# Key tiles transposed as fp32 pairs of bf16, with the order of TensorE's work pinned, in a decode attention kernel

**Chip, cores, metric.** One core of a Trainium2 chip. The metric is the device time of one execution in microseconds; executions are compared with those of the kernel before on the same chip. All runs quoted are of the state "fast".

## The reference, cut

```python
# A: B=4, Sq=1, D=512, 32 heads of 128, cache 8192 long, window W = 2048, all bf16
q = (xn @ wq)                                    # one query row per (batch, head): 128 pairs
k, v = k_cache[:, :, -2048:, :], v_cache[:, :, -2048:, :]
p = softmax(q @ k^T * 128**-0.5)
attn = (p @ v) @ wo
# B: a small MLP on the same 4 rows (w1..w4);  out = x + attn + mlp
```

The keys of one (batch, head) pair are 2048 x 128 bf16, 512 KB: 128 such tiles, 67.1 MB. The values are as much again. With 4.2 MB of wq, 4.2 MB of wo and the MLP's weights the core reads 146.5 MB. The score matmuls of this kernel sum over the partition dimension, so each key tile is transposed first, to bring the head dimension there.

## The kernel before, the parts concerned

```python
KV_BUFS, KTT_BUFS, STG_BUFS = 12, 16, 4       # key/value tiles, transposed halves, PSUM slots
Qm = qmpool.tile([P, NPAIR, QG], BF)          # per pair: 128x32, the query in one column, else 0

def emit_scores(h):                           # 16 matmuls, 4 rounds of 4 column strips (b)
    for sb in range(NSB):                     # NSB = 4 blocks of 512 keys
        c0 = sb * SBW
        sl, off = divmod(c0, SLW)
        for b in range(Bb):
            j = QG * b + h
            nc.tensor.matmul(S_ps[QG*b:QG*(b+1), c0:c0+SBW], lhsT=Qm[:, j, :],
                             rhs=ktT_tiles[(h, b)][sl][:, off:off+SBW],
                             start=(h == 0), stop=(h == Hq-1), tile_position=(0, QG*b))
    ...
for h in range(Hq):
    for b in range(Bb):
        kt = kvpool.tile([P, NCH, Dh], BF, name="kv")
        nc.sync.dma_start(out=kt[:], in_=kwin[b, h].rearrange("(p c) d -> p c d", c=NCH))
        slots = []
        for sl in range(NSLOT):               # 2 slots of 8 transposes
            stg = stgpool.tile([P, SLW], BF, name="stg")            # PSUM
            for cc in range(TPS):
                c = sl * TPS + cc
                nc.tensor.transpose(stg[:, cc*P:(cc+1)*P], kt[:, c, :], ident[:])
            ktT = kttpool.tile([P, SLW], BF, name="ktT")
            evac(ktT[:], stg[:])              # VectorE and ScalarE, 3:2
            slots.append(ktT)
        ktT_tiles[(h, b)] = slots
    if h - SCORE_LAG >= 0:                    # SCORE_LAG = 1
        emit_scores(h - SCORE_LAG)
# ... softmax over S_ps, then the value stage: o_ps <- PT, vt; combine; project with wo
```

The text is not the order in which TensorE gets the instructions: the framework reorders them when it builds the program.

Of the kernel before, what the change touches and what calls it, by code (L numbers as in the profile page):

```python
# [8 lines left out]
BF = mybir.dt.bfloat16  # L9
F32 = mybir.dt.float32  # L10
PSUM = bass.MemoryType.PSUM
ACTF = mybir.ActivationFunctionType
ALU = mybir.AluOpType
AX = mybir.AxisListType
# [5 lines left out]
STG_BUFS = 4  # L20
SCORE_LAG = 1
INCLUDE_TOKEN_MIX = True
TAIL_VSTAT_HEADS = 1
MLP_STAGE_AT = (10, 18, 44, 60)

# [2 lines left out]
def kernel(  # L28
# [14 lines left out]
    nc = tc.nc  # L43
    P = 128
    Bb, Sq, D = A_x.shape
    _, Hkv, Sk, Dh = A_k_cache.shape
    Hq = A_wq.shape[1] // Dh
    F = B_w3.shape[1]
    W = min(4096, max(256, Sk // 4))
    assert Sq == 1 and Dh == P and Hq == Hkv and Bb * Hq == P and D % P == 0  # L50
    assert W % P == 0
    NCH = W // P
    KD = D // P
    scale = float(Dh) ** -0.5
    NPAIR = Bb * Hq
    QG = P // Bb
    assert QG == 32 and Hq == QG
    SBW = min(512, W)
    NSB = W // SBW
    TPS = min(8, NCH)  # L60
    NSLOT = NCH // TPS
    SLW = TPS * P
# [3 lines left out]
    kwin = A_k_cache[:, :, Sk - W:Sk, :]  # L66
# [4 lines left out]
    def open_pool(**kw):  # L71
        cm = tc.tile_pool(**kw)
        return cm, cm.__enter__()

    def close_pool(cm):
        cm.__exit__(None, None, None)

    consts = ctx.enter_context(tc.tile_pool(name="consts", bufs=1))
    small = ctx.enter_context(tc.tile_pool(name="small", bufs=1))
    kvpool = ctx.enter_context(tc.tile_pool(name="kv", bufs=KV_BUFS))  # L80
    kttpool = ctx.enter_context(tc.tile_pool(name="ktt", bufs=KTT_BUFS))
    qmpool = ctx.enter_context(tc.tile_pool(name="qm", bufs=1))
# [5 lines left out]
    ident = consts.tile([P, P], BF)  # L88
    make_identity(nc, ident[:])
    eps_t = consts.tile([P, 1], F32)  # L90
    nc.vector.memset(eps_t[:], LN_EPS)
    Qm = qmpool.tile([P, NPAIR, QG], BF)
    nc.gpsimd.memset(Qm[:], 0.0)

    x_sb = small.tile([Bb, D], BF)
# [59 lines left out]
    stg_cm, stgpool = open_pool(name="stg", bufs=STG_BUFS, space=PSUM)  # L155
    ps0_cm, ps0 = open_pool(name="ps0", bufs=1, space=PSUM)
    xnT = small.tile([P, KD, Bb], BF)
    transpose_interleaved(xnT, xn_bf[:], Bb, KD, P, ps0, "xnT_ps")
    q_ps = ps0.tile([P, Hq * Bb], F32, name="q_ps")
    for h in range(Hq):  # L160
        for ic in range(KD):
            nc.tensor.matmul(q_ps[:, h * Bb:(h + 1) * Bb], lhsT=wq_sb[:, ic, h * Dh:(h + 1) * Dh],  # L162
                             rhs=xnT[:, ic, :], start=(ic == 0), stop=(ic == KD - 1))
    qm_diag = bass.AP(tensor=Qm.tensor, offset=Qm.offset,
                      ap=[list(Qm.ap[0]), [QG * QG, Bb], [QG + 1, Hq]])
    nc.vector.tensor_copy(out=qm_diag, in_=q_ps[:].rearrange("p (h b) -> p b h", b=Bb))  # L166
    close_pool(ps0_cm)
    close_pool(wq_cm)

    S_cm, spool = open_pool(name="S", bufs=1, space=PSUM)  # L170
    S_ps = spool.tile([P, W], F32, name="S_ps")

    order = [(i // Bb, i % Bb) for i in range(NPAIR)]
    evac_idx = [0]

    def evac(dst, src):
        k = evac_idx[0] % 5
        evac_idx[0] += 1
        if k in (0, 2, 4):
            nc.vector.tensor_copy(out=dst, in_=src)  # L180
        else:
            nc.scalar.copy(out=dst, in_=src)  # L182

    ktT_tiles = {}

    def emit_scores(h):
        for sb in range(NSB):
            c0 = sb * SBW
            sl, off = divmod(c0, SLW)
            for b in range(Bb):  # L190
                j = QG * b + h
                nc.tensor.matmul(S_ps[QG * b:QG * (b + 1), c0:c0 + SBW], lhsT=Qm[:, j, :],  # L192
                                 rhs=ktT_tiles[(h, b)][sl][:, off:off + SBW],
                                 start=(h == 0), stop=(h == Hq - 1), tile_position=(0, QG * b))
        for b in range(Bb):
            del ktT_tiles[(h, b)]

    for h in range(Hq):
        for b in range(Bb):
            kt = kvpool.tile([P, NCH, Dh], BF, name="kv")  # L200
            nc.sync.dma_start(out=kt[:], in_=kwin[b, h].rearrange("(p c) d -> p c d", c=NCH))
            slots = []
            for sl in range(NSLOT):
                stg = stgpool.tile([P, SLW], BF, name="stg")
                for cc in range(TPS):
                    c = sl * TPS + cc
                    nc.tensor.transpose(stg[:, cc * P:(cc + 1) * P], kt[:, c, :], ident[:])  # L207
                ktT = kttpool.tile([P, SLW], BF, name="ktT")
                evac(ktT[:], stg[:])
                slots.append(ktT)  # L210
            ktT_tiles[(h, b)] = slots
        if h - SCORE_LAG >= 0:
            emit_scores(h - SCORE_LAG)
    for h in range(max(0, Hq - SCORE_LAG), Hq):
        emit_scores(h)
# [9 lines left out]

    if INCLUDE_TOKEN_MIX:
        w1_sb = wpool.tile([P, KD, D], BF)
# [17 lines left out]
        weight_dma_at = {0: [dma_w3, dma_w4]}  # L245

    mx = smpool.tile([P, 1], F32)
    nc.vector.tensor_reduce(out=mx[:], in_=S_ps[:], axis=AX.X, op=ALU.max)  # L248
    nbias = smpool.tile([P, 1], F32)
    nc.vector.tensor_scalar(out=nbias[:], in0=mx[:], scalar1=-scale, scalar2=None, op0=ALU.mult)  # L250
    E = smpool.tile([P, W], F32)
    rowsum = smpool.tile([P, 1], F32)
    nc.scalar.activation(out=E[:], in_=S_ps[:], func=ACTF.Exp, bias=nbias[:], scale=scale, accum_out=rowsum[:])  # L253
    rinv = smpool.tile([P, 1], F32)
    nc.vector.reciprocal(out=rinv[:], in_=rowsum[:])
    Pn = smpool.tile([P, W], BF)
    nc.vector.tensor_scalar(out=Pn[:], in0=E[:], scalar1=rinv[:], scalar2=None, op0=ALU.mult)  # L257
    PT = smpool.tile([P, NCH, P], BF)
    for sl in range(NSLOT):
        ptp = stgpool.tile([P, SLW], BF, name="stg")  # L260
        for cc in range(TPS):
            c = sl * TPS + cc
            nc.tensor.transpose(ptp[:, cc * P:(cc + 1) * P], Pn[:, c * P:(c + 1) * P], ident[:])  # L263
        evac(PT[:, sl * TPS:(sl + 1) * TPS, :], ptp[:].rearrange("p (c j) -> p c j", j=P))
    close_pool(S_cm)
    close_pool(stg_cm)

# [5 lines left out]
    def mlp_stage1():  # L273
        if not INCLUDE_TOKEN_MIX:
            return
        xnn0 = small.tile([Bb, D], F32)
        layernorm(xnn0[:], xn[:], Bb)
        xnn0_bf = small.tile([Bb, D], BF)
        nc.vector.tensor_copy(out=xnn0_bf[:], in_=xnn0[:])
        xnn0T = small.tile([P, KD, Bb], BF)  # L280
        transpose_interleaved(xnn0T, xnn0_bf[:], Bb, KD, P, psB, "tpB")
        h1_ps = psB.tile([Bb, D], F32, name="mm512")
        for ic in range(KD):
            nc.tensor.matmul(h1_ps[:], lhsT=xnn0T[:, ic, :], rhs=w1_sb[:, ic, :], start=(ic == 0), stop=(ic == KD - 1))
        h1 = small.tile([Bb, Sq, D], BF)
        nc.scalar.activation(out=h1[:, 0, :], in_=h1_ps[:], func=ACTF.Gelu_apprx_tanh)
        st["h1"] = h1

    def mlp_stage2():
        if INCLUDE_TOKEN_MIX:  # L290
            h1 = st["h1"]
            g = small.tile([Bb, Sq, D], BF)
            nc.vector.memset(g[:], 0.0)
            cq = D // 4
            for s in range(Sq):
                for blk, sh in enumerate((-1, +1, -2, +2)):
                    ss = s + sh
                    if 0 <= ss < Sq:
                        nc.vector.tensor_copy(out=g[:, s, blk * cq:(blk + 1) * cq], in_=h1[:, ss, blk * cq:(blk + 1) * cq])
            gT = small.tile([P, KD, Bb], BF)  # L300
            transpose_interleaved(gT, g[:, 0, :], Bb, KD, P, psB, "tpB")
            hs_ps = psB.tile([Bb, D], F32, name="mm512")
            for ic in range(KD):
                nc.tensor.matmul(hs_ps[:], lhsT=gT[:, ic, :], rhs=w2_sb[:, ic, :], start=(ic == 0), stop=(ic == KD - 1))
            nc.vector.tensor_tensor(out=x1[:], in0=xn[:], in1=hs_ps[:], op=ALU.add)
        else:
            nc.vector.tensor_copy(out=x1[:], in_=xn[:])
        xnn = small.tile([Bb, D], F32)
        layernorm(xnn[:], x1[:], Bb)
        xnn_bf = small.tile([Bb, D], BF)  # L310
        nc.vector.tensor_copy(out=xnn_bf[:], in_=xnn[:])
        st["xnn_bf"] = xnn_bf
# [14 lines left out]
    def mlp_stage4():  # L327
# [3 lines left out]
        for fc in range(FCH):  # L331
# [15 lines left out]
                          in_=r32[:, 0:VG].unsqueeze(2).to_broadcast([P, VG, P]))  # L347
# [25 lines left out]
    for i in range(NPAIR):  # L373
        h, b = order[i]
        j = QG * b + h
# [4 lines left out]
        nc.sync.dma_start(out=vt[:], in_=vwin[b, h].rearrange("(p c) d -> p c d", c=NCH))  # L380
        if h >= Hq - TAIL_VSTAT_HEADS:
            if b == 0:
                oT_dir = otps_pool.tile([P, Bb], F32, name="oT_ps")
            for c in range(NCH):
                nc.tensor.matmul(oT_dir[:, b:b + 1], lhsT=vt[:, c, :], rhs=PT[:, c, j:j + 1],
                                 start=(c == 0), stop=(c == NCH - 1))
            if b == Bb - 1:
                head_epilogue_project(h, oT_dir)
        else:
# [3 lines left out]
            for g in range(NVG):  # L393
                nc.tensor.matmul(o_ps[QG * b:QG * b + VG, :], lhsT=PT[:, g * VG:(g + 1) * VG, j],  # L394
                                 rhs=vt[:, g * VG:(g + 1) * VG, :],
                                 start=(g == 0), stop=(g == NVG - 1), tile_position=(0, QG * b))
# [39 lines left out]
```

## Time and profile before

| | before |
|---|---|
| time, median of 6 runs | 396.59 us (395.27 to 399.32) |
| profiled span | 394.5 us |
| first to last key transpose | 16.4 to 208.3 us |
| last score ends, first value matmul starts | 210.1, 221.0 us |

The key stage goes from 16 to 210 us, softmax to 221, the value stage from there. A stage's limit is read from GB/s and from what the DMA's issue queue waits for.

### The profile page before, as it was taken

To read this page: it belongs to the slowest core of one execution; us is meant where nothing else is said; L and a number is where in the kernel's file an instruction comes from. 1 tells how busy PE (TensorE), PEld (TensorE's weight loads), DVE (VectorE), ACT (ScalarE), POOL (GpSimd) and SP (SyncE) were. 2 spreads that over 40 slices of the span, in tenths; PEclk is the share of its full clock that TensorE was granted. 3 is DMA by queue.
4 is the path that set the end of the run, shared out by engine and by line. 5 is a ranking of instruction groups with operands and counts; after the bars stand their busy time and mean duration, and the time that the engine had idled before them with its cause. 6 is when DMAs were issued, how large, how long until landed. Compare 5 with 4: busy or idle time off the path is not lost.

```text
span 394.5 us, 8101 instructions
## 1 busy us (share of the span) xinstructions
PE 304.7 (77%) x3416; PEld 178.0 (45%) x3416; DVE 188.0 (48%) x287; ACT 120.0 (30%) x149; POOL 4.3 (1%) x7
## 2 busy tenths in 40 slices
PE   0699999999999999999992865767466665666664
PEld 0666666666666766766761412222122222222222
DVE  5254555555555555555554444242544444444432
ACT  1155555554554564654554221100000000000000
POOL 4000000000000000000000000000000000000000
PEclk9999999999999999999998675855655555799996
DMA  8999999999999999999999599999999999999992
GB/s 326 412 408 407 408 406 407 367 331 365 335 375 356 333 357 358 328 362 354 339 405 387 207 403 393 408 372 389 410 402 410 407 410 410 407 410 410 407 410 112
DMA packets 43059, 147.00 MB, mean 373 GB/s; under 512 B 4264, under 2 KB 9744, under 8 KB 42768
## 3 DMA queue, kind: packets, MB, share of 16 engines
q1 hardware_dynamic: 43016, 146.49, 97.3%
q8 instruction: 26, 0.43, 0.4%
q14 instruction: 9, 0.07, 0.1%
q10 hardware_dynamic: 8, 0.00, 0.0%
HBM read 146.48 MB, written 0.00 MB: 371 GB/s over the span
## 4 chain that ended last, share of the span: by engine, by line
PE 67%; DVE 15%; DMA 14%; ACT 2%; issue 1%; DVEq 0%; ACTq 0%; SPq 0%
PE stg L207 30%; PE S_ps L192 15%; PE o_ps L394 13%; DMA kv<-in_A_v_cache_dram 10%; DVE o_sum L362 6%; DVE Dm L360 4%; DVE ktT L180 3%; PE oT_ps L364 3%; DMA wq_sb<-in_A_wq_dram 3%; PE mm L333 1%; PE y_ps L370 1%; PE q_ps L162 1%; PE mm L322 1%; DVE mx L248 1%; ACT E L253 1%
## 5 line engine op out<-in xcount | busy, mean ns | idle before, releaser
L180 DVE COPY ktT<-stg 128x1024 bf16<-128x1024 bf16 x154 | 104.1, 690 | 88.1 <-PE stg L207 80.4
L207 PEld LDWEIGHTS <-kv 128*128 128x128 bf16 x2048 | 116.2, 99 | 44.4 <-DMA kv<-in_A_k_cache_dram 27.9
L207 PE MATMUL stg<-ident,kv 128*128 128x128 bf16 x2048 | 135.7, 221 | 0.0
L182 ACT COPY ktT<-stg 128x1024 bf16<-128x1024 bf16 x102 | 102.2, 1012 | 99.5 <-PE stg L207 99.5
L394 PE MATMUL o_ps<-kv,PT 128*4 128x512 bf16 x496 | 83.4, 536 | 5.3 <-DMA kv<-in_A_v_cache_dram 4.8
L192 PE MATMUL S_ps<-ktT,Qm 128*32 128x512 bf16 x512 | 67.4, 385 | 5.2 <-DVE ktT L180 4.4
L360 DVE TENSOR_TENSOR Dm<-o_ps,maskD 128x512 f32<-128x512 f32 x31 | 21.4, 691 | 73.2 <-PE o_ps L394 73.2
L364 PE MATMUL oT_ps<-Sel,o_sum 128*128 128x4 f32 x62 | 15.7, 323 | 51.3 <-DVE o_sum L362 51.3
L369 ACT CAST oT_sb<-oT_ps 128x4 bf16<-128x4 f32 x32 | 5.2, 163 | 155.1 <-PE oT_ps L364 152.6
L364 PEld LDWEIGHTS oT_ps<-Sel,o_sum 128*128 128x128 f32 x62 | 13.0, 261 | 72.2 <-DVE o_sum L362 72.2
L394 PEld LDWEIGHTS <-PT 128*4 128x4 bf16 x496 | 23.7, 101 | 41.4 <-issue 35.3
L362 DVE TENSOR_REDUCE o_sum<-Dm 128x128 f32<-128x512 f32 x31 | 31.6, 1018 | 1.0
L192 PEld LDWEIGHTS <-Qm 128*32 128x32 bf16 x512 | 14.0, 94 | 18.7 <-issue 6.7
L370 PE MATMUL y_ps<-wo_sb,oT_sb 128*4 128x512 bf16 x32 | 17.3, 540 | 2.1 <-ACT oT_sb L369 2.1
L392 DVE MEMSET o_ps<- 128x512 f32 x31 | 15.0, 485 | 3.4 <-DVE PT L180 0.2
L162 PE MATMUL q_ps<-xnT,wq_sb 128*128 128x4 bf16 x128 | 3.6, 166 | 7.5 <-DMA wq_sb<-in_A_wq_dram 7.5
L263 PE MATMUL stg<-ident,Pn 128*128 128x128 bf16 x16 | 1.9, 312 | 7.5 <-DVE Pn L257 7.5
L162 PEld LDWEIGHTS <-wq_sb 128*128 128x128 bf16 x128 | 3.5, 104 | 7.6 <-DMA wq_sb<-in_A_wq_dram 7.6
L370 PEld LDWEIGHTS <-oT_sb 128*4 128x4 bf16 x32 | 3.2, 101 | 5.5 <-ACT oT_sb L369 5.5
L263 PEld LDWEIGHTS <-Pn 128*128 128x128 bf16 x16 | 1.6, 147 | 8.0 <-DVE Pn L257 8.0
L333 PE MATMUL mm<-w_sb,g3T 128*4 128x512 bf16 (+1 forms) x11 | 4.9, 611 | 0.0
L166 DVE CAST Qm<-q_ps 128x128 bf16<-128x128 f32 x1 | 0.7, 718 | 8.4 <-PE q_ps L162 8.4
(66 smaller groups left out, 49.7 us busy)
## 6 DMA issues: line engine op xcount, KB each, us to landing
kv<-in_A_k_cache_dram SPq DMA_DIRECT2D x128, 512.0 KB, 6.1
kv<-in_A_v_cache_dram SPq DMA_DIRECT2D x128, 512.0 KB, 10.1
wq_sb<-in_A_wq_dram SPq DMA_DIRECT2D x1, 4096.0 KB, 12.1
wo_sb<-in_A_wo_dram SPq DMA_DIRECT2D x4, 1024.0 KB, 11.1
w_sb<-in_B_w_dram SPq DMA_DIRECT2D x1, 1376.0 KB, 9.3
w_sb<-in_B_w_dram SPq DMA_DIRECT2D x1, 1280.0 KB
w_sb<-in_B_w_dram SPq DMA_DIRECT2D x2, 512.0 KB, 9.6
w_sb<-in_B_w_dram SPq DMA_DIRECT2D x1, 96.0 KB, 9.1
```

What stands on the lines that cost most here:

```text
L162: nc.tensor.matmul(q_ps[:, h * Bb:(h + 1) * Bb], lhsT=wq_sb[:, ic, h * Dh:(h + 1) * Dh], rhs=xnT[:, ic, :], start=(ic == 0), stop=(ic == K ...
L180: nc.vector.tensor_copy(out=dst, in_=src)
L182: nc.scalar.copy(out=dst, in_=src)
L192: nc.tensor.matmul(S_ps[QG * b:QG * (b + 1), c0:c0 + SBW], lhsT=Qm[:, j, :], rhs=ktT_tiles[(h, b)][sl][:, off:off + SBW], start=(h == 0), ...
L207: nc.tensor.transpose(stg[:, cc * P:(cc + 1) * P], kt[:, c, :], ident[:])
L333: nc.tensor.matmul(h2_ps[:], lhsT=g3T[:fw, fc, :], rhs=w4_sb[:fw, fc, :], start=(fc == 0), stop=(fc == FCH - 1))
L360: nc.vector.tensor_tensor(out=Dm[:], in0=o_ps[:], in1=maskD[:], op=ALU.mult)
L362: nc.vector.tensor_reduce(out=o_sum[:], in_=Dm[:].rearrange("p (m d) -> p d m", m=VG), axis=AX.X, op=ALU.add)
L364: nc.tensor.matmul(oT_ps[:], lhsT=o_sum[:], rhs=Sel[:], start=True, stop=True)
L370: nc.tensor.matmul(y_ps[:], lhsT=oT_sb[:], rhs=wo_sb[:, h, :], start=(h == 0), stop=(h == Hq - 1))
L392: nc.vector.memset(o_ps[:], 0.0)
L394: nc.tensor.matmul(o_ps[QG * b:QG * b + VG, :], lhsT=PT[:, g * VG:(g + 1) * VG, j], rhs=vt[:, g * VG:(g + 1) * VG, :], start=(g == 0), sto ...
```

## The change

The intent: read two neighbouring bf16 as one fp32 word, so that a key tile takes 8 fp32 transposes instead of 16. The head dimension then comes out split: partition i of a transposed tile holds elements 2i and 2i+1 of one key chunk (i < 64) or of the next (i >= 64), interleaved. The scores therefore use 64 rows, a step of two elements, and a query permuted to match. The diff's core (setup, masks and softmax views cut):

```diff
+    ident32 = consts.tile([P, P], F32)
+    make_identity(nc, ident32[:])
+    ... PermE, built from ident; Qm of twice the size
+    for e in range(2):
+        nc.tensor.matmul(qx_ps[:, e, :], lhsT=PermE[:, e, :], rhs=q_bf[:], start=True, stop=True)
...
+        def emit_scores(h):
+            for sl in range(NSLOT):
+                for e in range(2):
+                    for c2 in range(2):
+                        for b in range(Bb):
+                            ...
+                            rhs = src[HP*c2:HP*(c2+1), :].rearrange("i (x e) -> i x e", e=2)[:, :, e]
+                            col0 = c2 * SW2 + sl * NW
+                            tc.keep_in_program_order(nc.tensor.matmul(S_ps[QG*b:QG*(b+1), col0:col0+NW],
+                                             lhsT=Qm[HP*c2:HP*(c2+1), e, j, :], rhs=rhs,
+                                             start=(h == 0 and e == 0), stop=(h == Hq-1 and e == 1),
+                                             tile_position=(HP*c2, QG*b)))
...
+            kt32 = kt[:].rearrange("p c d -> p (c d)").bitcast(F32)
+            ...
+                    tc.keep_in_program_order(nc.tensor.transpose(stg[:, dc*P:(dc+1)*P],
+                                             kt32[:, cc*P:(cc+1)*P], ident32[:]))
```

Note the two `keep_in_program_order`: transposes and scores are also pinned to the order of the text.

More of the change, by code (lines that the diff above doesn't have):

```diff
@@ L22 @@
 INCLUDE_TOKEN_MIX = True
+PAIR_TRANSPOSE = True
 TAIL_VSTAT_HEADS = 1
@@ L91 @@
     nc.vector.memset(eps_t[:], LN_EPS)
-    Qm = qmpool.tile([P, NPAIR, QG], BF)
+    HP = P // 2
+    if PAIR_TRANSPOSE:
+        assert NCH % 2 == 0
+        ident32 = consts.tile([P, P], F32)
+        make_identity(nc, ident32[:])
+        PermE = consts.tile([P, 2, P], BF)
+        id_eo = ident[:].rearrange("p (x two) -> p two x", two=2)
+        for e in range(2):
+            for c2 in range(2):
+                nc.vector.tensor_copy(out=PermE[:, e, c2 * HP:(c2 + 1) * HP], in_=id_eo[:, e, :])
+        Qm = qmpool.tile([P, 2, NPAIR, QG], BF)
+    else:
+        Qm = qmpool.tile([P, NPAIR, QG], BF)
     nc.gpsimd.memset(Qm[:], 0.0)
@@ L163 @@
                              rhs=xnT[:, ic, :], start=(ic == 0), stop=(ic == KD - 1))
-    qm_diag = bass.AP(tensor=Qm.tensor, offset=Qm.offset,
-                      ap=[list(Qm.ap[0]), [QG * QG, Bb], [QG + 1, Hq]])
-    nc.vector.tensor_copy(out=qm_diag, in_=q_ps[:].rearrange("p (h b) -> p b h", b=Bb))
+    if PAIR_TRANSPOSE:
+        q_bf = small.tile([P, Hq * Bb], BF)
+        nc.vector.tensor_copy(out=q_bf[:], in_=q_ps[:])
+        qx_ps = ps0.tile([P, 2, Hq * Bb], F32, name="qx_ps")
+        for e in range(2):
+            nc.tensor.matmul(qx_ps[:, e, :], lhsT=PermE[:, e, :], rhs=q_bf[:], start=True, stop=True)
+            qm_diag = bass.AP(tensor=Qm.tensor, offset=Qm.offset + e * NPAIR * QG,
+                              ap=[list(Qm.ap[0]), [QG * QG, Bb], [QG + 1, Hq]])
+            nc.vector.tensor_copy(out=qm_diag, in_=qx_ps[:, e, :].rearrange("p (h b) -> p b h", b=Bb))
+    else:
+        qm_diag = bass.AP(tensor=Qm.tensor, offset=Qm.offset,
+                          ap=[list(Qm.ap[0]), [QG * QG, Bb], [QG + 1, Hq]])
+        nc.vector.tensor_copy(out=qm_diag, in_=q_ps[:].rearrange("p (h b) -> p b h", b=Bb))
     close_pool(ps0_cm)
@@ L170 @@
     S_cm, spool = open_pool(name="S", bufs=1, space=PSUM)
-    S_ps = spool.tile([P, W], F32, name="S_ps")
     order = [(i // Bb, i % Bb) for i in range(NPAIR)]
@@ L184 @@
     ktT_tiles = {}
-    def emit_scores(h):
-        for sb in range(NSB):
-            c0 = sb * SBW
-            sl, off = divmod(c0, SLW)
-            for b in range(Bb):
-                j = QG * b + h
-                nc.tensor.matmul(S_ps[QG * b:QG * (b + 1), c0:c0 + SBW], lhsT=Qm[:, j, :],
-                                 rhs=ktT_tiles[(h, b)][sl][:, off:off + SBW],
-                                 start=(h == 0), stop=(h == Hq - 1), tile_position=(0, QG * b))
-        for b in range(Bb):
-            del ktT_tiles[(h, b)]
@@ L198, with s_col, transpose_tile, emit_scores @@
-    for h in range(Hq):
-        for b in range(Bb):
-            kt = kvpool.tile([P, NCH, Dh], BF, name="kv")
-            nc.sync.dma_start(out=kt[:], in_=kwin[b, h].rearrange("(p c) d -> p c d", c=NCH))
+    if PAIR_TRANSPOSE:
+        NDC = NCH // 2
+        DPS = min(4, NDC)
+        NSLOT = NDC // DPS
+        NW = DPS * P
+        SW2 = max(W // 2, 512)
+        S_ps = spool.tile([P, 2 * SW2], F32, name="S_ps")
+        S_valid = S_ps[:].rearrange("p (c x) -> p c x", c=2)[:, :, 0:W // 2]
+        def s_col(chunk):
+            c2, q = chunk % 2, chunk // 2
+            return c2 * (W // 2) + q * P
+        def emit_scores(h):
+            for sl in range(NSLOT):
+                for e in range(2):
+                    for c2 in range(2):
+                        for b in range(Bb):
+                            j = QG * b + h
+                            src = ktT_tiles[(h, b)][sl]
+                            rhs = src[HP * c2:HP * (c2 + 1), :].rearrange("i (x e) -> i x e", e=2)[:, :, e]
+                            col0 = c2 * SW2 + sl * NW
+                            tc.keep_in_program_order(nc.tensor.matmul(S_ps[QG * b:QG * (b + 1), col0:col0 + NW],
+                                             lhsT=Qm[HP * c2:HP * (c2 + 1), e, j, :], rhs=rhs,
+                                             start=(h == 0 and e == 0), stop=(h == Hq - 1 and e == 1),
+                                             tile_position=(HP * c2, QG * b)))
+            for b in range(Bb):
+                del ktT_tiles[(h, b)]
+        def transpose_tile(kt):
+            kt32 = kt[:].rearrange("p c d -> p (c d)").bitcast(F32)
+            slots = []
+            for sl in range(NSLOT):
+                stg = stgpool.tile([P, DPS * P], F32, name="stg")
+                for dc in range(DPS):
+                    cc = sl * DPS + dc
+                    tc.keep_in_program_order(nc.tensor.transpose(stg[:, dc * P:(dc + 1) * P], kt32[:, cc * P:(cc + 1) * P], ident32[:]))
+                ktT = kttpool.tile([P, 2 * DPS * P], BF, name="ktT")
+                evac(ktT[:], stg[:].bitcast(BF))
+                slots.append(ktT)
+            return slots
+    else:
+        S_ps = spool.tile([P, W], F32, name="S_ps")
+        S_valid = S_ps[:]
+        def s_col(chunk):
+            return chunk * P
+        def emit_scores(h):
+            for sb in range(NSB):
+                c0 = sb * SBW
+                sl, off = divmod(c0, SLW)
+                for b in range(Bb):
+                    j = QG * b + h
+                    nc.tensor.matmul(S_ps[QG * b:QG * (b + 1), c0:c0 + SBW], lhsT=Qm[:, j, :],
+                                     rhs=ktT_tiles[(h, b)][sl][:, off:off + SBW],
+                                     start=(h == 0), stop=(h == Hq - 1), tile_position=(0, QG * b))
+            for b in range(Bb):
+                del ktT_tiles[(h, b)]
+        def transpose_tile(kt):
@@ L210 @@
                 slots.append(ktT)
-            ktT_tiles[(h, b)] = slots
+            return slots
+    for h in range(Hq):
+        for b in range(Bb):
+            kt = kvpool.tile([P, NCH, Dh], BF, name="kv")
+            nc.sync.dma_start(out=kt[:], in_=kwin[b, h].rearrange("(p c) d -> p c d", c=NCH))
+            ktT_tiles[(h, b)] = transpose_tile(kt)
         if h - SCORE_LAG >= 0:
@@ L247 @@
     mx = smpool.tile([P, 1], F32)
-    nc.vector.tensor_reduce(out=mx[:], in_=S_ps[:], axis=AX.X, op=ALU.max)
+    nc.vector.tensor_reduce(out=mx[:], in_=S_valid, axis=(AX.XY if PAIR_TRANSPOSE else AX.X), op=ALU.max)
     nbias = smpool.tile([P, 1], F32)
@@ L252 @@
     rowsum = smpool.tile([P, 1], F32)
-    nc.scalar.activation(out=E[:], in_=S_ps[:], func=ACTF.Exp, bias=nbias[:], scale=scale, accum_out=rowsum[:])
+    E_v = E[:].rearrange("p (c x) -> p c x", c=2) if PAIR_TRANSPOSE else E[:]
+    nc.scalar.activation(out=E_v, in_=S_valid, func=ACTF.Exp, bias=nbias[:], scale=scale, accum_out=rowsum[:])
     rinv = smpool.tile([P, 1], F32)
@@ L258 @@
     PT = smpool.tile([P, NCH, P], BF)
-    for sl in range(NSLOT):
-        ptp = stgpool.tile([P, SLW], BF, name="stg")
-        for cc in range(TPS):
-            c = sl * TPS + cc
-            nc.tensor.transpose(ptp[:, cc * P:(cc + 1) * P], Pn[:, c * P:(c + 1) * P], ident[:])
-        evac(PT[:, sl * TPS:(sl + 1) * TPS, :], ptp[:].rearrange("p (c j) -> p c j", j=P))
+    PTG = (2 * DPS) if PAIR_TRANSPOSE else TPS
+    for g0 in range(0, NCH, PTG):
+        if PAIR_TRANSPOSE:
+            ptp = stgpool.tile([P, DPS * P], F32, name="stg")[:].bitcast(BF)
+        else:
+            ptp = stgpool.tile([P, SLW], BF, name="stg")[:]
+        for cc in range(PTG):
+            c = g0 + cc
+            nc.tensor.transpose(ptp[:, cc * P:(cc + 1) * P], Pn[:, s_col(c):s_col(c) + P], ident[:])
+        evac(PT[:, g0:g0 + PTG, :], ptp.rearrange("p (c j) -> p c j", j=P))
     close_pool(S_cm)
```

## The prediction

> **What bounds the kernel now.** First the slices of the page, then the stretches view, then single instructions in the timeline. Each slice is 394.5/40 = 9.9 us; the key cache streams through slices 2 to 21, the value cache from 22 on.
>
> ```profile
> PE   0699999999999999999992865767466665666664
> PEclk9999999999999999999998675855655555799996
> DMA  8999999999999999999999599999999999999992
> GB/s 326 412 408 407 408 406 407 367 331 365 335 375 356 333 357 358 328 362 354 339 405 387 207 403 393 408 372 389 410 402 410 407 410 410 407 410 410 407 410 112
> ```
>
> The DMA row says 9 nearly everywhere, so it doesn't tell what limits; the bytes do. For six slices the queue moves 407 GB/s, then only about 350 until the keys end, then 207 for one slice, then 400 to 410. PE is at 9 exactly while the rate is low. The stretches show it in microseconds:
>
> ```profile
> 20.00:60.00 40.00, 38.83 (x530) 26.81 (x530) 21.57 (x32) 21.01 (x22) 0.00 (x0) 1.00 1.03 408
> 100.00:140.00 40.00, 39.10 (x542) 26.86 (x539) 21.96 (x33) 21.48 (x23) 0.00 (x0) 1.00 0.97 348
> 300.00:340.00 40.00, 24.75 (x169) 9.28 (x160) 17.60 (x25) 1.30 (x8) 0.00 (x0) 0.50 1.03 409
> ```
>
> (Columns: length, PE, weight loads, VectorE, ScalarE, GpSimd, granted clock, DMA share, GB/s.) PE is 97% busy from the start, at full clock; the DMA runs ahead of it only until its 12 buffers are full (408 GB/s), then waits for buffers (348). With the values PE is busy 62% at half clock and the DMA stays at 409. So the key stage is bound by PE and the value stage by the DMA. The queue's own waits agree:
>
> ```profile
> SPq L201 <- PE stg L207: 110.9, 105, 1.4
> ```
>
> The issue of key tiles waited 110.9 us for PE transposes to free a buffer. By tile: first transpose at 16.3 us, last at 208.3, so 192/127 = 1.51 us a tile, where the DMA needs 524,288 B / 408 GB/s = 1.285 us. PE's timeline shows what the 1.51 us are:
>
> ```profile
> 108.57 1.07 PE L207 MATMUL stg<-ident,kv 128*128 128x128 bf16 x16
> 109.57 0.61 PE L192 MATMUL S_ps<-ktT,Qm 128*32 128x512 bf16 x7
> 110.11 1.07 PE L207 MATMUL stg<-ident,kv 128*128 128x128 bf16 x16
> ```
>
> A tile starts every 1.54 us here. One transpose lasts 0.22 us as a record, so 16 that span 1.07 start (1.07 - 0.22)/15 = 57 ns apart. Eight score matmuls (one record of these is missing) take 0.61 us and, elsewhere in the timeline, four take 0.40: each further four, which sit side by side in four column strips, add 0.21 us. The rest, about 0.15 us before and 0.1 us after the scores, is the change between the two shapes.
>
> After the keys comes a serial piece, and the end:
>
> ```profile
> 208.86 1.20 PE S_ps L192 x13
> 210.09 2.30 DVE mx L248
> 220.98 3.83 PE o_ps L394 x22
> ```
>
> Softmax is 10.9 us from the last score to the first value matmul. In it the DMA refills the 12 buffers and stops (slice 23, 207 GB/s).
>
> [...] in the fp32 pair of L364:
>
> ```profile
> 387.57 0.30 PEld L364 LDWEIGHTS oT_ps<-Sel,o_sum 128*128 128x128 f32 x2 [2.34 <-DVE o_sum L362]
> L207 PEld LDWEIGHTS <-kv 128*128 128x128 bf16 x2048 | 116.2, 99 | 44.4 <-DMA kv<-in_A_k_cache_dram 27.9
> ```
>
> The shortest fp32 load there lasts 186 ns against 99 for bf16, and two span 0.30 us: the second starts 0.11 us after the first. At half clock they are slower still. [...] The trace shows four at once in the 128x32 form, none in 64x32. [...] No strided moving operand is in this trace.
>
> **The change, part by part.**
>
> *Transposes.* 16 bf16 transposes a tile become 8 of fp32 (a pair of bf16 is carried as one word). The built program holds one weight load and one matmul for each, 1024 in all, so they are not split in two as L364's are. The key data is the stationary operand, so each needs an fp32 weight load[...]. If the 128-column stream (57 ns) overlaps the next load, as it does for bf16, eight cost 0.86 us against 16 x 57 = 0.91. So halving the count saves almost nothing by itself; PE becomes bound by loads instead of streams.
>
> *Scores.* Even and odd halves of the head dimension now lie in different words, so a tile needs 8 matmuls of 64 rows instead of 4 of 128 rows. If eight tiles of 64x32 run at once, a head (4 tiles) still needs four rounds: 4 x 0.21 + 0.18 of drain = about 1.0 us. If only four run at once, eight rounds: 1.8 us.
>
> *Order.* The program order of PE is now pinned: 32 transposes, then 32 scores of the head before. Read from the built program, it holds for all heads. Before, the shape changed once a tile; now once a head, so 0.25 us a tile becomes 0.06. This is the real saving.
>
> *Evacuation.* Still 256 copies of 128x1024 bf16 at 690 ns (VectorE) and 1012 ns (ScalarE) in a 3:2 split: five take about 2.07 us, eight (a head) 3.3 us. Transposes deliver a slot every 4 x 107 = 0.43 us, the copies take 0.41 each: with four slots they keep pace, with small stalls that I put at 0.2 us a head.
>
> *Start.* A second identity, a query tile of twice the size cleared on GpSimd (4.3 us of busy time becomes about 8), two permutation matmuls and one more copy: all behind the 12 us load of wq but for about 1 us, and the first tiles wait in buffers anyhow.
>
> Sum for PE a head: 32 x 107 = 3.4, plus scores 1.0, changes 0.25, stalls 0.2: 4.9 us, 1.2 us a tile. That is under the DMA's 1.285 (5.14 a head), so the key stage becomes DMA-bound: it ends for the DMA at 12 + 128 x 1.285 = 176.5 us, and the last score at about 181 instead of 210.
>
> *The rest.* Value loads need the buffers that the keys free, now at once. After 176.5 the queue has 2 MB of weights and 12 value tiles to move, 8.4 MB or 20 us, so until 197; softmax ends at 181 + 11 = 192. The gap of slice 23 (about 4 us lost) closes too. Then the whole kernel is one stream: 146.5 MB / 408 GB/s = 359 us, plus about 2 lost at the start, 2 for gaps, and 7 from the last landing to the end (DMA share falls at about 387 of 394.5). Span 370, and the measured median lies 2.1 us above the profiled span: 372. For the chance of a slower scores part I name 374.
>
> **The rivals.** *Four at once instead of eight in the scores (or the strided read at half speed).* PE needs 3.4 + 1.8 + 0.25 + 0.2 = 5.65 a head, 1.41 a tile; keys end near 16.5 + 181 + 2 = 199, ten us before the old time: about 384. For it: nothing shows eight. Against: four columns do overlap fully. If both happen, 1.8 a tile, keys end near 250: about 435.
> [...]
> *The clock.* PE will now idle for about 5% and stream for half of each transpose; the trace shows 0.5 in the value stage at 62% busy. If the keys fell to half clock, [...] PE would be bound again. Against: being bound, it would be busy, and 97% busy kept 1.00.
> *No gain because the DMA was at 9 tenths all along.* The rates refute it: 348 against 408 GB/s.
>
> **Range and chances.** The floor is 359 + 9 + 2 = 370, 368 at 410 GB/s. I give 0.75 to the fp32 transpose at about 107 ns with scores at full or half speed (372 to 386, all over 2% faster), 0.07 to a mild loss that ends within 2%, 0.18 to the slow forms. Predicted 374, range 367 to 402.
>
> **What would show it.** Right: about 407 GB/s through all slices of the keys, the last score near 181 us, fp32 transposes starting 107 ns apart, groups of eight scores 0.21 us apart, the queue's wait for transposes mostly gone, PE at 9 or a little less with clock 1.00. Wrong: transposes 160 ns or more apart, eight scores 0.4 us apart, clock below 1 in the keys, or the last score early and the end late because the value stage starves or slows.

## The result, and the profile after

| | before | after |
|---|---|---|
| median | 396.9 us (16 runs) | 373.66 us (8 runs, 373.47 to 374.97) |
| ratio | | 0.9414, 95% interval 0.9392 to 0.9436 |
| profiled span | 394.5 us | 371.6 us |
| first, last key transpose | 16.4, 208.3 us | 18.2, 180.4 us |
| last score ends | 210.1 us | 182.7 us |
| first value matmul | 221.0 us | 193.6 us |

A ratio here is the mean time of one kernel's fast runs over that of the other's of the same rounds, so not quite the ratio of the medians quoted. The output passed the comparison with the reference. The comparison says little of the scores, though: with these inputs they have a spread of about 0.05 x 0.05 = 0.0025, so softmax is nearly flat.

The slices of the page after (9.3 us each):

```profile
PE   0499999999899999999638575577666766666664
PEclk9999999999999999999956676565999999999996
GB/s 339 397 407 408 407 408 408 407 407 407 408 409 407 407 409 407 408 408 405 390 398 397 416 396 400 368 396 403 407 410 410 410 409 409 410 407 409 410 402 97
```

The low stretch of the keys and the 207 of the softmax gap are gone; the stream never stops. The stretches, in the columns of the prediction:

```profile
20.00:60.00 40.00, 39.42 (x497) 32.39 (x495) 26.36 (x40) 26.59 (x28) 0.00 (x0) 1.00 1.03 408
100.00:140.00 40.00, 36.84 (x483) 28.61 (x489) 24.57 (x38) 23.83 (x26) 0.00 (x0) 1.00 1.03 407
300.00:340.00 40.00, 26.27 (x147) 9.63 (x146) 17.56 (x24) 1.30 (x8) 0.00 (x0) 1.00 1.03 409
```

In the middle of the keys the rate went from 348 to 407 GB/s, and PE's busy time fell below its former 39.1 because it now waits. The issue queue's waits turned over:

```profile
SPq L281 <- DMA kv<-in_A_k_cache_dram: 109.5, 120, 2.4
SPq L281 <- PE stg L242: 14.4, 57, 0.3
```

The queue that had waited 110.9 us for transposes now waits 14.4 us for them and 109.5 us for earlier transfers. PE's timeline:

```profile
104.96 2.85 PE L242 MATMUL stg<-ident,kv 128*128 128x128 f32 x24
108.02 1.07 PE L242 MATMUL stg<-ident,kv 128*128 128x128 f32 x8 [0.21 <-DMA kv<-in_A_k_cache_dram]
109.02 1.10 PE L228 MATMUL S_ps<-ktT,Qm 64*32 64x512 bf16 x32
```

Eight transposes span 1.07 us, one record 0.273 us: (1.07 - 0.27)/7 = 0.11 us apart. All 32 scores of a head take 1.10 us, and the last tile of the head is waited for at the DMA.

Where the time went: softmax starts 27.4 us earlier, and the kernel ends 22.9 us earlier. The other 4.5 us are not lost to anything new. In both kernels the value stage ends with the last landing: the last packet of the caches comes at 389.3 us before and 366.5 after, and the last value matmul ends at 390.6 and 367.7. Before, the DMA had run ahead while PE lagged, so at the first value matmul less was left to move: 65.9 MB by the trace's packets, 69.0 after (173.6 us to the end, 178.0 after). The gain is the DMA time that was not used: before, the low slices and the gap; after, none.

### The profile page after: what moved, and what is told of

The parts are those of the page before. It is cut to its first block, busy times and chain, and to the rows that moved or that the text cites.

```text
span 371.6 us, 7217 instructions
## 1 busy us (share of the span) xinstructions
PE 281.9 (76%) x2906; PEld 174.6 (47%) x2906; DVE 191.7 (52%) x293; ACT 118.4 (32%) x149; POOL 8.0 (2%) x9
## 4 chain that ended last, share of the span: by engine, by line
DMA 72%; PE 18%; DVE 6%; ACT 1%; issue 1%; SPq 0%; ACTq 0%; DVEq 0%
DMA kv<-in_A_k_cache_dram 39%; DMA kv<-in_A_v_cache_dram 30%; PE o_ps L470 6%; PE stg L242 4%; DMA wq_sb<-in_A_wq_dram 3%; DVE o_sum L438 2%; DVE Dm L436 1%; PE oT_ps L440 1%; PE mm L409 1%; PE S_ps L228 1%; PE q_ps L175 1%; PE y_ps L446 1%; PE mm L398 1%; DVE mx L319 1%; ACT E L325 1%
## 5 line engine op out<-in xcount | busy, mean ns | idle before, releaser
L242 PE MATMUL stg<-ident,kv 128*128 128x128 f32 x1024 | 126.7, 278 | 6.9 <-DMA kv<-in_A_k_cache_dram 6.7
L242 PEld LDWEIGHTS stg<-ident,kv 128*128 128x128 f32 x1024 | 111.5, 142 | 29.4 <-issue 12.8
L470 PE MATMUL o_ps<-kv,PT 128*4 128x512 bf16 x496 | 92.2, 448 | 12.4 <-DMA kv<-in_A_v_cache_dram 11.8
L470 PEld LDWEIGHTS <-PT 128*4 128x4 bf16 x496 | 28.7, 93 | 57.7 <-issue 44.4
L440 PE MATMUL oT_ps<-Sel,o_sum 128*128 128x4 f32 x62 | 13.4, 286 | 41.2 <-DVE o_sum L438 41.2
L440 PEld LDWEIGHTS oT_ps<-Sel,o_sum 128*128 128x128 f32 x62 | 10.7, 216 | 54.6 <-DVE o_sum L438 53.8
L228 PE MATMUL S_ps<-ktT,Qm 64*32 64x512 bf16 x1024 | 35.2, 388 | 0.0
L228 PEld LDWEIGHTS <-Qm 64*32 64x32 bf16 x1024 | 12.0, 90 | 12.2 <-issue 5.2
L446 PE MATMUL y_ps<-wo_sb,oT_sb 128*4 128x512 bf16 x32 | 14.2, 443 | 1.8 <-ACT oT_sb L445 1.8
L106 POOL MEMSET Qm<- 128x8192 bf16 x1 | 6.9, 6925 | 0.0
```

The costliest lines, as they stand in the source:

```text
L106: nc.gpsimd.memset(Qm[:], 0.0)
L228: tc.keep_in_program_order(nc.tensor.matmul(S_ps[QG * b:QG * (b + 1), col0:col0 + NW], lhsT=Qm[HP * c2:HP * (c2 + 1), e, j, :], rhs=rhs, s ...
L242: tc.keep_in_program_order(nc.tensor.transpose(stg[:, dc * P:(dc + 1) * P], kt32[:, cc * P:(cc + 1) * P], ident32[:]))
L440: nc.tensor.matmul(oT_ps[:], lhsT=o_sum[:], rhs=Sel[:], start=True, stop=True)
L446: nc.tensor.matmul(y_ps[:], lhsT=oT_sb[:], rhs=wo_sb[:, h, :], start=(h == 0), stop=(h == Hq - 1))
L470: nc.tensor.matmul(o_ps[QG * b:QG * b + VG, :], lhsT=PT[:, g * VG:(g + 1) * VG, j], rhs=vt[:, g * VG:(g + 1) * VG, :], start=(g == 0), sto ...
```

## The experiments

Two parts of the change could be the cause: the pairing (fewer transposes, other scores) and the pinned order. The prediction said that pairing "saves almost nothing by itself" and that the order, 32 transposes then 32 scores instead of a change of shape once a tile, "is the real saving". The tests separate them. First the order itself, as the built programs list it (T transposes, S scores):

```
before: T32 S1 T16 S2 T32 S7 T16 S7 T16 S2 T16 S2 T16 S8 T16 S4 T16 S2 T16 S2 T16 S8 ...
after:  T64 S32 T32 S32 T32 S32 ...
```

### Order alone: bf16 transposes as before, but pinned

```diff
-                    nc.tensor.transpose(stg[...], kt[:, c, :], ident[:])
+                    tc.keep_in_program_order(nc.tensor.transpose(stg[...], kt[:, c, :], ident[:]))
-                nc.tensor.matmul(S_ps[...], ...)
+                tc.keep_in_program_order(nc.tensor.matmul(S_ps[...], ...))
```

> The kernel before, with bf16 transposes and 128-row scores as they were, but its transposes and scores pinned in program order: 64 transposes, then 16 scores, once a head. If the order is the saving (my theory): a head costs PE 64 x 57 ns + 1.0 us scores + 0.25 us change of shape + 0.2 us stalls = 5.1 us, 1.27 us a tile, just at the DMA's 1.285; time 373 to 379 us, last score near 182 us, 400 GB/s or more through the keys. If the fp32 pairing is the saving (rival): about 396 us, as before.

Measured: 375.11 us (374.9 to 376.16), ratio 0.9467, interval 0.9441 to 0.9493. The last score ended at 184.1 us.

```profile
123.50 1.07 PE L207 MATMUL stg<-ident,kv 128*128 128x128 bf16 x16 [0.21 <-DMA kv<-in_A_k_cache_dram]
124.50 1.05 PE L192 MATMUL S_ps<-ktT,Qm 128*32 128x512 bf16 x16
100.00:140.00 40.00, 38.23 (x627) 30.87 (x628) 25.07 (x38) 24.82 (x26) 0.00 (x0) 1.00 1.03 407
```

Without any pairing PE waits for the DMA and the rate is 407 GB/s. Two added calls give 21 of the change's 23 us.

### Pairing alone: the kernel after without the pinned order

```diff
-                            tc.keep_in_program_order(nc.tensor.matmul(S_ps[...], ...))
+                            (nc.tensor.matmul(S_ps[...], ...))
-                    tc.keep_in_program_order(nc.tensor.transpose(stg[...], ...))
+                    (nc.tensor.transpose(stg[...], ...))
```

> The kernel after, with pairing, but without the pinned order: the scheduler then breaks transposes and scores into runs of about 8 and 8, with some runs of 1 to 4 or 9 to 11 scores. If the order is the saving: 1.35 to 1.5 us a tile, 380 to 392 us. If the pairing is the saving: 374 us as after.

Measured: 396.22 us (395.21 to 397.84), ratio 0.9998, interval 0.996 to 1.0036: nothing of the gain is left, where I had expected 380 to 392 us. PE's timeline:

```profile
123.55 0.62 PE L228 MATMUL S_ps<-ktT,Qm 64*32 64x512 bf16 x9
124.10 1.09 PE L242 MATMUL stg<-ident,kv 128*128 128x128 f32 x8
125.12 0.81 PE L228 MATMUL S_ps<-ktT,Qm 64*32 64x512 bf16 x4
125.86 1.09 PE L242 MATMUL stg<-ident,kv 128*128 128x128 f32 x8
```

The second and third lines are one tile: 1.76 us, from 124.10 to 125.86. Its run of four scores takes 0.81 us, where a run of eight elsewhere in the timeline takes 0.42. From first to last transpose it is 1.511 us a tile, the same as before.

### Shape changes or torn rounds? One whole round after each tile

The scheduler's order has two faults: it changes shape often, and it tears rounds (runs of 1, 2, 3, 5 or 7 scores where 4 belong side by side). Two kernels keep the frequent changes but no tearing. On the kernel after:

```diff
-        if h - SCORE_LAG >= 0:
-            emit_scores(h - SCORE_LAG)
+            if h - SCORE_LAG >= 0:
+                emit_scores(h - SCORE_LAG, (b,))     # after tile b: round b alone, 8 scores
```

> The kernel after, pinned, but one whole round of 8 scores after each tile's 8 transposes instead of 32 after 32: the same work and four times the changes of shape. From the trace after, a change costs 0.20 us from last transpose to first score and 0.34 back. Per tile 7 x 0.109 + 0.20 + 0.03 + 0.34 = 1.33 us, a little over the DMA's 1.285: 375 to 381 us, last score 186 to 190. If changes of shape cost nothing: 374, last score 182. If it is as slow as the unpinned order, the tearing of rounds isn't the cause.

Measured: 380.75 us (380.27 to 380.96), ratio 0.9602, interval 0.9579 to 0.9626; the last score ended at 194.8 us, 1.375 us a tile: a little more than the 1.33 worked out, with the last score later than the 186 to 190 expected. The same edit on the pinned bf16 kernel, four scores after each tile:

> The kernel before, pinned, but with one whole round of 4 scores after each tile's 16 transposes: as many changes of shape as before, no torn round. From the traces: 15 x 57 ns + 0.15 + 0.33 + 0.03 = 1.36 us a tile at most. If tearing is most of the old loss: near 1.35 us a tile, 377 to 383 us. If the number of shape changes is most of it: near the old 1.51 us, 390 to 397.

Measured: 374.97 us (374.7 to 376.18), ratio 0.9464, interval 0.9447 to 0.9482, at 1.340 us a tile: the pace expected, and a time below the 377 to 383 expected.

```profile
101.99 1.07 PE L207 MATMUL stg<-ident,kv 128*128 128x128 bf16 x16
102.98 0.40 PE L194 MATMUL S_ps<-ktT,Qm 128*32 128x512 bf16 x4
103.31 1.07 PE L207 MATMUL stg<-ident,kv 128*128 128x128 bf16 x16
```

These are no fewer changes of shape than before (123 runs of scores against 113), and nearly all of the gain is there. So the number of changes alone does not make the old kernel slow; what the scheduler puts into its runs does: torn rounds, and scores ahead of the copies that they need (below). At 1.34 us a tile PE is slower than the DMA (1.285), but the last score ends at 188.3 us and the stream hardly dips: 350 GB/s from 200 to 210 us, where the kernel after has 418. At 1.375 it dips to 241 there (380.75 us). That the 12 buffers of run-ahead hide the smaller lag is read from these rates, not tested.

PE's side, from its single records: the time from the last transpose before each run of scores to the first transpose after it, summed.

| kernel | runs of scores | sum | mean of a run |
|---|---|---|---|
| before | 113 | 81.2 us | 0.72 us |
| bf16, round after each tile | 123 | 59.2 us | 0.48 us |
| bf16, pinned once a head | 30 | 33.9 us | 1.13 us |
| paired, unpinned | 125 | 84.8 us | 0.68 us |
| paired, round after each tile | 123 | 67.9 us | 0.55 us |
| paired, after | 30 | 37.2 us | 1.24 us |

Row 1 to row 2 is what the scheduler put into the runs, 22.0 us, although row 2 has ten runs more; row 2 to row 3 is the changes of shape, 25.3 us for 93 fewer, 0.27 us each, of which 0.06 is the last transpose's own interval. In the paired kernel the same two steps are 16.9 us and 30.7 us (0.33 each, 0.11 of it the transpose's). How a torn round costs shows in the kernel before:

```profile
93.13 0.78 PE L192 MATMUL S_ps<-ktT,Qm 128*32 128x512 bf16 x2
93.84 1.07 PE L207 MATMUL stg<-ident,kv 128*128 128x128 bf16 x16
95.24 0.39 PE L192 MATMUL S_ps<-ktT,Qm 128*32 128x512 bf16 x2 [0.34 <-DVE ktT L180]
```

Two scores take 0.78 us where a whole round of four takes 0.40: the second starts 0.40 us after the first and waits on VectorE's count, for the copy of a tile just transposed. In the next run PE sat 0.34 us for such a copy. In the built program 83 of the scores' waits stand inside a run, 4 in the one pinned once a head, and the 512 scores need 167 rounds instead of 128. How the 22 us divide between extra rounds and these waits was not separated.

### Does it matter that eight scores run side by side?

> The kernel after, the same 32 scores a head, but all of row half 0 first and then all of row half 1[...]. If eight side by side matter as I worked out: eight rounds instead of four, 0.8 us more a head, 5.6 us, 1.4 us a tile, last score near 198 us, time 382 to 388. If the scores are hidden or not concurrent anyway: 374.

```diff
-            for sl in range(NSLOT):
-                for e in range(2):
-                    for c2 in range(2):
+            for c2 in range(2):
+                for sl in range(NSLOT):
+                    for e in range(2):
```

Measured: 373.74 us (373.44 to 374.8), ratio 0.9432: no loss, against my expectation. Either PE had slack or the order of the program was not the order of work.

```profile
124.18 1.14 PE L228 MATMUL S_ps<-ktT,Qm 64*32 64x512 bf16 x32
```

The built program does list 16 scores of one half and then 16 of the other. The trace's records don't carry the row position, but the 32 scores still took 1.28 us from transpose to transpose (1.24 in the kernel after), not the two that eight rounds need, and they start in groups of four, 0.05 and 0.18 us apart in turn. So I took away the second half itself:

```diff
-  rhs = src[HP*c2:HP*(c2+1), :]...   lhsT=Qm[HP*c2:HP*(c2+1), e, j, :]   tile_position=(HP*c2, QG*b)
+  rhs = src[0:HP, :]...              lhsT=Qm[0:HP, e, j, :]              tile_position=(0, QG*b)
```

> The kernel after with every score matmul on row half 0 (wrong result on purpose, the same number of instructions), so that no two halves can run side by side, whatever the order. If the earlier run with the halves in sequence was fast because the hardware overlapped the halves all the same: here eight rounds of 0.22, scores 1.9 us a head instead of 1.1, 1.35 to 1.45 us a tile, 380 to 388 us. If PE simply has that much slack beside the DMA: 374.

Measured: 386.39 us (385.95 to 387.25), ratio 0.9749, interval 0.9735 to 0.9764.

```profile
102.16 3.82 PE L242 MATMUL stg<-ident,kv 128*128 128x128 f32 x32
105.91 2.01 PE L228 MATMUL S_ps<-ktT,Qm 64*32 64x512 bf16 x32
100.00:140.00 40.00, 40.00 (x459) 29.56 (x461) 22.79 (x36) 22.51 (x23) 0.00 (x0) 1.00 1.00 376
```

The same 32 scores on one half take 2.01 us instead of 1.10, and 2.14 from transpose to transpose, where the run before this one took 1.28. So the kernel after does run eight at once, it needs that, and the run before this one must have overlapped the halves although the program lists one after the other.

### PE's own pace, with the DMA out of the way

Half of every key tile is loaded and transposed twice; the result is wrong.

```diff
-   nc.sync.dma_start(out=kt[:], in_=kwin[b, h].rearrange(...))
+   nc.sync.dma_start(out=kt[:, 0:NCH // 2, :], in_=kwin[b, h].rearrange(...)[:, 0:NCH // 2, :])
-   ... kt32[:, cc*P:(cc+1)*P] ...
+   ... kt32[:, dc*P:(dc+1)*P] ...         # in the bf16 kernel: kt[:, cc, :] for kt[:, c, :]
```

> The kernel after with half of every key tile loaded and transposed twice (wrong result on purpose): PE, VectorE and ScalarE do the same work, the DMA needs 0.65 us a tile, so PE's own pace shows. My sum: 4.9 us a head, last score near 16.5 + 157 + 2 = 175 us (range 172 to 180), time 362 to 370. If PE had much slack (3.7 us a head or less): last score before 140.

> The pinned kernel with bf16 transposes, half of every key tile loaded and transposed twice (wrong result on purpose). My sum: 5.1 us a head, last score near 16.5 + 163 + 2 = 182 us (178 to 186), so 5 to 8 us after that of the paired kernel treated the same way. If pairing saves PE nothing: the same last score as there. If it saves half of the transposes' time: 40 us or more later.

Measured: paired, 343.98 us, last score at 172.0 us; bf16 and pinned, 340.84 us, last score at 168.2 us. The first is at the early edge of what I expected (172 to 180), the second below it (178 to 186). The paired kernel's time is some 20 us below the 362 to 370 expected: at its first value matmul 61 MB were left to move, where the kernel after has 69. The paired kernel's head, then the bf16 one's:

```profile
104.63 3.72 PE L242 MATMUL stg<-ident,kv 128*128 128x128 f32 x32
108.28 1.11 PE L228 MATMUL S_ps<-ktT,Qm 64*32 64x512 bf16 x32
```

```profile
102.03 3.75 PE L207 MATMUL stg<-ident,kv 128*128 128x128 bf16 x64
105.70 1.05 PE L192 MATMUL S_ps<-ktT,Qm 128*32 128x512 bf16 x16
```

Thirty-two fp32 transposes take as long as sixty-four of bf16. From first to last transpose it is 1.193 us a tile paired and 1.176 us not, so pairing costs PE about 1.5% in place of saving anything. My order of the two was wrong, since each term of the bf16 sum was too large: transposes 64 x 0.056 = 3.58 us a head (I had 3.65), scores with their change 1.13 - 0.06 = 1.07 (1.25), stalls 0.08 (0.2). A stall here is what a gap between two transposes has over the usual 56 or 109 ns, as a mean of all heads.

### A version better than both?

The kernels pinned once a head are bound by the stream (407 to 408 GB/s from 20 to 170 us), so only its end is left. The chain after the last landing passes through VectorE's combining of head 30:

```diff
-TAIL_VSTAT_HEADS = 1
+TAIL_VSTAT_HEADS = 2
```

> The changed kernel itself, unchanged, on the chip of the next two, so that they can be compared with it: 373 to 375 us.

> The kernel after with the last two heads' values, instead of the last one's, multiplied straight into the output column (a constant of the kernel, 1 to 2), so that the combining chain of head 30 on VectorE no longer stands between the last landing and the end. In the profile after that chain holds PE from 362 to 365.9 us. Expected: 0.5 to 1.5 us less than after, 372 to 373.5 us; if the end hangs on the last landing alone: the same time.

> The kernel before with the pinned order and the same two tail heads, without pairing. If pairing is worth nothing beside the order: within 0.5% of the paired one with two tail heads, so 373 to 375 us.

Measured in the same rounds: 373.8 us (373.37 to 374.8) unchanged, ratio 0.9423; 373.7 us (373.53 to 373.79) with two tail heads, ratio 0.9417, interval 0.9396 to 0.9439; 374.77 us (374.73 to 375.05) for bf16 pinned with two tail heads, ratio 0.9446. So no gain. With two tail heads the end looks like this:

```profile
365.90 0.59 PE L461 MATMUL oT_ps<-PT,kv 128*128 128x1 bf16 x16 [0.67 <-DMA kv<-in_A_v_cache_dram]
367.16 0.58 PE L461 MATMUL oT_ps<-PT,kv 128*128 128x1 bf16 x16 [0.67 <-DMA kv<-in_A_v_cache_dram]
```

PE now sits before each of the last tiles until it lands, the last at about 367.1 us, and copy, projection, sum and store follow as before. The VectorE chain had stood beside the last landings and not in their way. No version beats the kernel after clearly; the bf16 kernel with the two pins comes within 0.4% of it. That 0.4% (375.11 against 373.74 us for the halves-in-sequence kernel of the same rounds) has no cause that these runs show.

## Why the prediction was right

**What bounds what.** Right. The key stage was PE's at 1.51 us a tile and became the DMA's: 348 to 407 GB/s, and the queue's wait for transposes fell from 110.9 to 14.4 us. Its account of what fills the 1.51 us was not right (below).

**Transposes at 107 ns, bound by the fp32 weight load.** Right in the pace: 109 ns, and 1024 instructions. What the trace of before shows for it is the fp32 pair of L364: at a granted clock of 1.00 its second load starts 108 ns after the first. The reason, that the loads set the pace, is not shown, and the start of the traces speaks against it. The clock records begin with a granted clock of 1.00, at 19.7 us in the trace before and 21.3 us in the one after. Earlier, bf16 transposes start 107 ns apart (56 later) and fp32 ones 213 (109 later), so TensorE worked there at about half its later pace; no record names the clock. The loads of L364, with only four columns to stream, start 165 ns apart where the granted clock is 0.50 and 108 where it is 1.00. If the loads compare, something slower than the load holds the fp32 transposes at the slow pace (213 against 165). At both paces their step is about twice the bf16 one (213 against 2 x 107, 109 against 2 x 56), while a record lasts 273 ns against 219; what sets it was not shown. At full clock twice the bf16 step (112) and the step of the loads (108) are nearly equal, so the number held whichever it was; in that it was lucky. "Halving the count saves almost nothing" is shown by three runs: pairing alone 0.9998, order alone 0.9467, and equal PE pace with the DMA out of the way.

**Scores, eight at once, about 1.0 us a head.** Right: 1.10 us, and 2.01 when eight cannot run. The strided operand cost little, if anything: rounds start 0.23 us apart, 0.22 in the pinned bf16 kernel.

**"This is the real saving", the shape changes.** Right in kind, but about half of PE's saving in the bf16 kernel and two thirds in the paired one. The prediction counted 0.25 us a change; measured 0.27 (bf16). It did not see that the scheduler also tore the rounds and put scores ahead of their copies, 22.0 us of the 47.3 us that pinning took from the score parts of the bf16 kernel (81.2 - 33.9). The timeline of before had it in view: a run of two scores lasting longer than one of four. It also explained two signs away. It took runs of seven for eight with a record missing, but the page has all 512 scores, and the built program lists runs of seven. Its 1.54 us tile counts eight scores, where a tile has four on average (512/128): 16 x 0.057 + 0.21 + 0.25 = 1.37 us, not 1.51. The missing 0.14 us is 18 us over 128 tiles. The sum for the changed kernel was built from its own parts, so this gap did not reach the number. With the tearing gone, the changes of shape need not have gone for the bf16 kernel's gain.

**The sum, 4.9 us a head.** Measured 1.193 x 4 = 4.8 us with the DMA out of the way. By terms: transposes 32 x 0.109 = 3.49 us (3.42 predicted), scores with their change 1.24 - 0.11 = 1.13 (1.25), stalls 0.18 as a mean of all heads (0.2).

**Start.** Sized too small: the first transpose came 1.8 us later (18.2 against 16.4), not 1 us. It cost nothing, as the tiles waited in their buffers.

**The rest.** Last score 182.7 us against 181, softmax's gap closed, one stream to the end, span 371.6 us against 370. Two of its terms were off and cancel in part: the last packet of the caches lands at 366.5 us, 7.4 after the 359 of the bare stream (4 predicted), and from there to the end it is 5.1 us (7 predicted). The sum gave 372; the extra 2 us in the named 374 covered the chance of slow scores, which did not occur, so the exact hit of the median is partly luck.

**The rivals.** Half-speed scores and a lower clock in the keys (rounds 0.23 us apart, clock 1.00 from 21 us on) are refuted by the trace after. Four scores at once instead of eight came as a run of its own, with one half alone: last score 200.0 us, 386.39 us, where the prediction had about 199 and 384. One slip had no effect: value tiles are issued from 194 us on, slice 20 and not 22.

## What to carry to other kernels

When a scheduler orders the work, read the order before you optimise the instructions: look for short runs that last longer than long ones, and for waits inside a group that should start together. Pin the order alone first; here that was two calls and gave nearly all that a rewrite of the transposes gave. And test each part of a change by itself: this one's headline part was worth nothing without the pins.
